# Pairwise channel-layer tails, a residual turned by DMA, and a bias-on-TensorE first batch in an attention and MLP-mixer kernel

## The chip, the core and the metric

The kernel runs on one core of one Trainium2 chip. The metric is device time in microseconds (us) of one execution; ten runs of the kernel before have a median of 291.51 us (290.18 to 292.82). Engines: PE is TensorE (matrix products into PSUM), ACT is ScalarE, DVE is VectorE, POOL is GpSimd, SP is SyncE. Loads that cast f32 to bf16 are issued by POOL, plain and transposing DMAs by SP.

## What is computed

For each of 8 batches: sliding-window attention with a linear distance bias (8 heads of 64, 576 positions, a window of 128), then one mixer block over tokens and one over channels.

```python
scores = scale * q @ k.T                                  # 8 x 576 x 576 a batch
bias = slopes[h] * -abs(i - j); mask = (0 <= i - j < 128)
attn = softmax(where(mask, scores + bias, -1e9))
x = (attn @ v) laid out as [576, 512]
u = x + (relu(x.T @ w_tok1) @ w_tok2).T                   # 576 -> 256 -> 576
out = u + relu(u @ w_ch1) @ w_ch2                         # 512 -> 1536 -> 512
```

## The kernel before, in words

**Tiling.** The 576 positions of a batch are four blocks of 128 and a tail of 64. The softmax needs no maximum: the scores are exponentiated on ACT (`pe`), and DVE multiplies them by `masks`, which holds exp(-slope * distance), zero outside the window (`pb`). A 65th column of ones in the values (`vp`) gives the row sums.

**Work items.** Each item is a small function with a one-letter name, and strings of names (PROLOGUE, FIRST, SECOND, PERIOD, LAST) set by hand the order in which every engine gets its instructions. A prime moves an item to the next batch. Names that are used below:

- `l`, `q`: loads of k and q of batches 0 and 1 (batch 0's heads 0 to 3 by SP as f32, cast by DVE in `cq` and ACT in `ck`; the rest by POOL); `v0` to `v4`: values; `LW`: the token weights W1, W1t, W2; `G0` to `G2`, `H0`, `H1`: the channel weights WC1 and WC2.
- `A0` to `A3`, `AT`: q and k of two heads, or of the tail, transposed on PE into `psM` banks (line 229), and copied out by DVE and ACT (line 234). Later batches are transposed by DMA (`Zq`, `Zk`).
- `S<kb><j>`: scores of key block kb for four heads (lines 308 to 317), their exponential on ACT (line 322, 279 for the half items `s`, `t`) and the mask product on DVE (lines 282, 329, 333, 338). Score matmuls use 64 of the 128 array rows, two heads at a time.
- `P`: attention times values and the normalising; in batch 0 `p0` to `p3`, each for two heads. `k`, `u`, `x` in batch 0 (`K`, `U`, `X` elsewhere): first token layer, second token layer with residual, transpose for the channel layers. `UT`: the tail of the second token layer, into `utt` (channels x 64 positions for each batch of a pair).
- `C0` to `C11`: first channel layer, one 128-wide block of the 1536 each (line 501, four matmuls of 512 columns), ReLU on DVE (line 504) or ACT (line 507). `C` needs every `x` of its batch.
- `T0`, `T1` (lines 510 to 521): the same layer for the 64-position tail, six blocks each, in **every** batch: 24 matmuls with 64 columns into the single bank `psT`, then one ReLU on ACT (line 519).
- `D<c><part>`: second channel layer for 128 positions, in three parts of four matmuls (line 549), a DVE add of the residual (line 554) and the store. `E0` to `E2`: the same for the two tails of a pair of batches together (line 571); at its end four matmuls against the identity (line 575) bring the residual from `utt`, and ACT copies the bank out (line 579).
- `M0` to `M3`: the mask tables (two ACT exponentials each, line 703); `W<n>`: n warm-up matmuls on zeros (line 687); `e1`, `e2`, `ek`, `ex`: constants in buffers, written by ACT.

**Order and rotation.** PSUM holds two double banks `psS` (scores and P), three banks `psM` in rotation (A, C, D, E, K, U, X, some S of batch 0), and `psT`. Each engine takes its instructions in the order of the strings, so an instruction that waits holds back what stands behind it. POOL issues its DMAs in that order too, and each waits until the eighth one before it has landed.

Of the kernel before, what the change touches and what calls it, by code (L numbers as in the profile page):

```python
# [10 lines left out]
ACT = mybir.ActivationFunctionType  # L11
# [8 lines left out]
U_ACT = (0, 1, 3)  # L20
# [3 lines left out]
l0 I W2 q0 q1 J M3 l1 ck0 M0 W3 M1 W3 W3 l23 cq0 O qt m0 A0 q23 W3 v3 v0 ck1 v1 M2 FC W1 cq1 A1  # L24
s0 v2 S20 A2 t0 AT S10 A3 W2 S30 W2 S11 l01' v4 S01 q01' LW ex p0 G0 p1 W1 S21 m1 k0 S31 k1 q23'
l23' A1' e1 qt' W2 v4' ek p2 u0 A0' p3 G1 k2 S00' LC G2 u1 v1'
"""
FIRST = """
H1 v3' k3 u2 v2' x0 u3 A3' v0' W1 H0 A2' Lk'' UT x2 x1 AT' Lq'' S20' x3 Zq'' Zk'' Lk''' T0 S10'
S01' v3'' v0'' Lq''' C9 v0''' S21' C11 v4'' C3 e2 S31' C0 C5 S30' C7 C8 S11' C10 E0 C1 C2 v2''  # L30
C4 P2' v4''' C6 P3' D00 P0' P4' T1 E2 v1'' P1' D01 D02 K0' K1' D10 U1' v2''' D11 D12 U2' UT'
Zq''' X1' U0' U3' D20 D30 S11'' S20'' v1''' D21 D31 E1 Zk''' S00'' D22 S01'' D32
"""
SECOND = """
T1 X2 X0 X3 S30' S31' T0 C8 C9 C7 C11 C2 P0' C5 Lk''' C3 v0''' C4 v1''' C1 S21' S10' C10 Lq'''
v2''' v3'' C0 P4' C6 D00 P3' D01 v3''' P1' P2' D02 K0' S20'' K1' v4''' S01'' D10 D11 D12 U1' U0'
UT' U2' U3' X0' S21'' S11'' D20 D21 X3' S10'' S00'' E0 E1 D22 E2 X2' D30 D31 X1' D32 P0''
"""
PERIOD = """
C3 C7 Zq'' S31' S30' C10 C1 Zk'' C8 P1' C6 T1 P2' C11 P4' C2 C4 P3' C9 Lk''' v4''' C0 C5 K0'  # L40
S00'' K1' S01'' D00 v0''' D01 D02 U2' T0 Lq''' v1''' U1' U0' UT' U3' P0'' D20 X3' v2''' X2'
v3''' X0' D10 X1' D21 D22 S11'' S10'' D11 D30 D31 E0 D12 D32 E1 E2 S21'' S20''
"""
LAST = """
C8 C0 C3 C4 C7 C11 T1 C10 C9 T0 C6 C2 C1 C5 D00 E0 D01 D02 D10 D11 E1 D20 D12 E2 D21 D30 D31 D22
D32
# [3 lines left out]
SPLIT = (1, 2)  # L50
S_M = (0, 2, 4, 5, 6)
S_P = ()
x_DVE = (1, 2, 3)
k_DVE = (2,)
AK_DVE = (2, 3, 7)
AQ_ACT = (1, 3, 4, 5, 7)
DVE_RELU = (2, 3, 4, 5, 7, 8, 10, 11)
# [3 lines left out]
def kernel(  # L61
# [31 lines left out]
    def T(name, shape, dt=bf16):  # L93
        return sb.tile(shape, dt, name=name, tag=name)
# [11 lines left out]
    def S2():  # L106

        t = psS[srot[0] % 2]
        srot[0] += 1
        return t  # L110
# [12 lines left out]
    dist = T("dist", [P, 2, P], f32)  # L123

# [32 lines left out]
    r2t = [T(f"r2t{i}", [P, NHT, 2, ST]) for i in range(2)]  # L157
    ob = [T(f"ob{i}", [P, DM], f32) for i in range(4)]
# [5 lines left out]
    def later(n, fn):  # L164
        pend.append([n, fn])
# [98 lines left out]

    def score_half(kb, a):

        def f():
            if a == 0:
                n = qrot[0]
                qrot[0] += 1  # L270
                half[kb] = (S2(), pe[n % len(pe)], pb[n % len(pb)])
                probs[0, kb, 0] = half[kb][2]
            s, e, p = half[kb]
            cs = slice(a * 256, (a + 1) * 256)
            for h in range(2):
                r = slice(h * D, (h + 1) * D)
                nc.tensor.matmul(s[:, h, cs], lhsT=kT[0][r, kb, a, :],
                                 rhs=qT[0][r, kb:kb + 2, a, :], start=True, stop=True)
            nc.scalar.activation(out=e[:, :, cs], in_=s[:, :, cs], func=ACT.Exp, scale=scale)

            def g():
                nc.vector.tensor_tensor(
                    out=p[:, :].rearrange("p (h x) -> p h x", h=2)[:, :, cs], in0=e[:, :, cs],
                    in1=masks[:, 0, :, a].rearrange("p h g x -> p h (g x)"), op=ALU.mult)
            later(MASK_LATER, g)
        return f
    tok1_banks = {}

    def score(b, kb, j):
# [4 lines left out]

        def f():
            n = qrot[0]
            qrot[0] += 1
            apart = j * 4 + kb in (S_M if b == 0 else S_P if b > 2 else ())
# [20 lines left out]
            split = apart or b == 0 and j * 4 + kb in SPLIT  # L319
# [6 lines left out]
            def g():  # L326
                if kb < NC - 1:
                    for h in (parts if b == 0 else (slice(0, 2),)):
                        nc.vector.tensor_tensor(  # L329
                            out=p[:, :].rearrange("p (h x) -> p h x", h=2)[:, h], in0=e[:, h, :],  # L330
                            in1=masks[:, j, h].rearrange("p h g a x -> p h (g a x)"), op=ALU.mult)
                    return
                nc.vector.tensor_tensor(
                    out=p[:, 0:512].rearrange("p (h g x) -> p h g x", h=2, g=2),
                    in0=e[:, :, 0:256].rearrange("p h (g x) -> p h g x", g=2),
                    in1=masks[:, j, :, :, 0, :], op=ALU.mult)

                nc.vector.tensor_tensor(
                    out=p[:, 512:1024].rearrange("p (u h x) -> p h u x", u=4, h=2),
                    in0=e[:, :, 256:512].rearrange("p h (u x) -> p h u x", u=4),  # L340
                    in1=maskt[:, j].rearrange("p h t g x -> p h (t g) x"), op=ALU.mult)
            later(MASK_LATER, g)
        return f
# [166 lines left out]
    def ch1_tail(b, g, n=6):  # L510
        def f():
            for j in range(n):
                ht = g * n + j
                o = psT[:, j * ST:(j + 1) * ST]
                for cb in range(NCB):
                    nc.tensor.matmul(o, lhsT=WC1[:, cb, ht * P:(ht + 1) * P],  # L516
                                     rhs=utt[(b // 2) % 2][:, cb, b % 2, :],
                                     start=(cb == 0), stop=(cb == NCB - 1))
            nc.scalar.activation(out=r2t[(b // 2) % 2][:, g * n:(g + 1) * n, b % 2, :],  # L519
                                 in_=psT[:, 0:n * ST].rearrange("p (j x) -> p j x", j=n),  # L520
                                 func=ACT.Relu)
        return f
# [36 lines left out]
    def ch2_tail(b, parts=2):  # L559

        st = {}
        pi2 = (b // 2) % 2

        def part(pi):
            def f():
                if pi == 0:
                    st["t"] = M()
                t = st["t"]
                n = NHT // parts
                for ht in range(pi * n, (pi + 1) * n):  # L570
                    nc.tensor.matmul(t[:, :], lhsT=r2t[pi2][:, ht, :, :], rhs=WC2[:, ht, :],  # L571
                                     start=(ht == 0), stop=False)
                if pi == parts - 1:
                    for cb in range(NCB):
                        nc.tensor.matmul(t[:, cb * P:(cb + 1) * P], lhsT=utt[pi2][:, cb, :, :],
                                         rhs=ident[:, :], start=False, stop=(cb == NCB - 1))
                    o = ob[orot[0] % len(ob)]
                    orot[0] += 1
                    nc.scalar.copy(out=o[:, :], in_=t[:, :])
                    for i in range(2):  # L580
                        nc.sync.dma_start(out=out[b - 1 + i, SM:S, :], in_=o[i * ST:(i + 1) * ST, :])
            return f
        return [part(i) for i in range(parts)]
# [107 lines left out]
    def ones_v(i):  # L691
        nc.vector.memset(vp[i][:, :, :, D:D + 1], 1.0)
        nc.vector.memset(vp[i][ST:P, NC, :, 0:D + 1], 0.0)
# [28 lines left out]

    def load_wc1(g):
        nc.gpsimd.dma_start(
            out=WC1[:, :, g * 512:(g + 1) * 512],
            in_=moe_w_ch1[:, g * 512:(g + 1) * 512].rearrange("(j p) h -> p j h", p=P))

    def first_constants():
        nc.vector.memset(kT[0][:, NC, :, ST:P], 0.0)
        nc.vector.memset(hm[:, :], 0.0)  # L730
        nc.vector.memset(hm[0:D, 0:1], 1.0)
        nc.vector.memset(hm[D:P, 1:2], 1.0)
# [5 lines left out]
    def fill_v(i):  # L738

        nc.scalar.activation(out=vp[i][:, :, :, D:D + 1].rearrange("p c h o -> p (c h o)"),  # L740
                             in_=zt[:, 0:(NC + 1) * H], func=ACT.Copy, bias=1.0)
        nc.scalar.copy(out=vp[i][ST:P, NC, :, 0:D + 1],
                       in_=zt[ST:P, None, 0:D + 1].broadcast_to([ST, H, D + 1]))

    def fill_k1():
        nc.scalar.copy(out=kT[1][:, NC, :, ST:P], in_=zt[:, None, 0:ST].broadcast_to([P, NHP, ST]))

    def fill_x1():
        nc.scalar.copy(out=xt[1][:, :].rearrange("p (a x) -> p a x", a=4),
                       in_=zt[:, None, :].broadcast_to([P, 4, P]))  # L750
# [16 lines left out]
    def names(b):  # L767
# [16 lines left out]
        for g in range(2):  # L784
            d[f"T{g}"] = ch1_tail(b, g)
# [22 lines left out]
        if b == 0:  # L808
# [13 lines left out]
            d["e1"], d["e2"] = lambda: fill_v(1), lambda: fill_v(2)  # L822
# [3 lines left out]
            d["LW"] = load_w12  # L826
            d["O"] = lambda: ones_v(0)
# [57 lines left out]
```

The softmax here doesn't subtract the row's maximum and nothing guards it: scores larger than these inputs give would overflow.

## Time and profile before

| | |
|---|---|
| median of ten runs | 291.51 us |
| the profiled execution | 291.71 us, span 290.0 us |
| mean granted PE clock | 0.994 |
| DVE busy | 177.4 us (61%), 348 instructions |
| ACT busy | 115.3 us (40%), 176 instructions |
| line 501 (C), line 549 (D) on PE | 384 and 372 matmuls, 90.2 and 86.5 us |
| line 516 (T) on PE | 384 matmuls of 64 columns, 13.8 us |
| line 687 (warm-up) on PE | 23 matmuls, 8.9 us |
| POOL's DMA queue | 17.41 MB, 78.2% of 16 DMA engines' span |
| first matmul of C | 35.30 us after the span's start |

Busy time counts each instruction from its start to its modelled end; matmuls overlap, so on PE the distance from one start to the next says more than the mean duration. Items have no names in the profile: they are found by line, by tile and by order. The chain that ended last goes back from the last instruction, at each step to what released it.

### The profile page before, as it was taken

The numbers are of one execution on the slowest core, as the hardware profiler recorded it, in microseconds if no ns is written. First come the engines' busy times: TensorE is split into PE (matmuls) and PEld (weight loads), VectorE is DVE, ScalarE is ACT, GpSimd is POOL, SyncE is SP. The second block draws the span as 40 slices with busy tenths as digits, with TensorE's granted clock in tenths as the row PEclk, the third lists the DMA queues.
The fourth block names the chain that finished last, engine by engine and source line by source line (L and its number), as shares of the span: only waits on it lengthen the run. The fifth ranks groups of instructions, "written<-read, shape, count | busy, mean of one in ns | idle before, by whom it ended". The sixth has DMA issues, their size and how long they took to land.

```text
span 290.0 us, 6456 instructions
## 1 busy us (share of the span) xinstructions
PE 281.1 (97%) x2707; PEld 155.5 (54%) x2707; DVE 177.4 (61%) x348; ACT 115.3 (40%) x176; POOL 99.4 (34%) x128
## 2 busy tenths in 40 slices
PE   8769999999999999999999999999999999999995
PEld 3348746546465556644655456644655456645543
DVE  3795687557687578456856467557846476426212
ACT  5878782137224632425341262435241263101300
POOL 8866543089319604920195006910000000000000
PEclk9998999999999999999999999999999999999999
DMA  7999999799999988997599679996703320051004
GB/s 176 165 199 193 198 184 139 152 161 140 149 184 153 171 205 109 138 182 158 125 123 169 125 178 116 139 161 159 128 2 90 98 67 2 36 111 72 2 36 145
DMA packets 148636, 38.00 MB, mean 131 GB/s; under 512 B 135808, under 2 KB 144128, under 8 KB 148608
## 3 DMA queue, kind: packets, MB, share of 16 engines
q0 software_dynamic: 103152, 17.41, 78.2%
q1 hardware_dynamic: 45456, 20.19, 30.4%
q8 instruction: 21, 0.34, 0.5%
q14 instruction: 7, 0.06, 0.1%
HBM read 35.85 MB, written 9.44 MB: 156 GB/s over the span
## 4 chain that ended last, share of the span: by engine, by line
PE 90%; DMA 4%; DVE 3%; issue 1%; POOL 1%; ACT 0%; SPq 0%
PE psM L501 29%; PE psM L549 28%; PE psM L434 4%; PE psM L459 4%; PE psS L308 4%; PE psT L516 4%; PE psM L571 4%; DMA W<-in_moe_w_tok_dram 3%; PE psS L373 2%; PE psS L369 2%; PE psS L401 1%; DMA qf<-in_q_dram 1%; PE psS L312 1%; PE psM L530 1%; PE psM L229 1%
## 5 line engine op out<-in xcount | busy, mean ns | idle before, releaser
L501 PE MATMUL psM<-utb,WC 128*128 128x512 bf16 x384 | 90.2, 379 | 0.0
L549 PE MATMUL psM<-WC,r 128*128 128x512 bf16 x372 | 86.5, 379 | 0.0
L322 ACT ACTIVATE pe<-psS 128x1024 bf16<-128x1024 f32 (+1 forms) x60 | 58.5, 1011 | 50.6 <-PE psS L308 44.3
L549 PEld LDWEIGHTS <-r 128*128 128x128 bf16 x372 | 34.5, 98 | 40.8 <-issue 3.2
L501 PEld LDWEIGHTS <-WC 128*128 128x128 bf16 x384 | 34.5, 97 | 37.7 <-issue 1.9
L504 DVE TENSOR_SCALAR r<-psM 128x512 bf16<-128x512 f32 x64 | 43.4, 687 | 15.0 <-PE psM L501 14.5
L185 POOL DMA_DIRECT2D kn<-in_k_dram x24 | 21.0, 893 | 80.0 <-DMA kT<-kn 75.1
L329 DVE TENSOR_TENSOR pb<-pe,masks 128x1024 bf16<-128x1024 bf16 (+1 forms) x52 | 32.8, 638 | 22.9 <-ACT pe L322 22.0
L554 DVE TENSOR_TENSOR ob<-psM,ub 128x512 f32<-128x512 f32 x31 | 21.4, 691 | 32.1 <-PE psM L549 32.0
L507 ACT ACTIVATE r<-psM 128x512 bf16<-128x512 f32 x32 | 19.1, 598 | 54.4 <-PE psM L501 53.8
L185 POOL DMA_DIRECT2D vp<-in_v_dram x32 | 29.2, 965 | 2.1 <-DMA WC<-in_moe_w_ch_dram 1.5
L185 POOL DMA_DIRECT2D qn<-in_q_dram x24 | 21.4, 947 | 3.4 <-DMA WC<-in_moe_w_ch_dram 2.9
L383 DVE TENSOR_TENSOR xb<-psS,rt 128x512 bf16<-128x512 f32 x28 | 19.4, 692 | 1.0
L461 DVE TENSOR_TENSOR ub<-psM,xb 128x512 bf16<-128x512 f32 x28 | 18.0, 685 | 2.1 <-PE psM L459 1.8
L373 PE MATMUL psS<-vp,pb 128*128 128x65 bf16 x224 | 15.7, 193 | 0.0
L373 PEld LDWEIGHTS <-pb 128*128 128x128 bf16 x224 | 13.6, 97 | 3.3
L459 PE MATMUL psM<-r,W 128*128 128x512 bf16 x56 | 15.4, 379 | 0.0
L516 PEld LDWEIGHTS <-WC 128*128 128x128 bf16 x384 | 13.2, 98 | 3.1
L519 ACT ACTIVATE r2t<-psT 128x384 bf16<-128x384 f32 x16 | 7.9, 491 | 17.4 <-PE psT L516 16.8
L308 PE MATMUL psS<-qT,kT 64*128 64x256 bf16 x172 | 14.5, 272 | 0.0
L516 PE MATMUL psT<-utt,WC 128*128 128x64 bf16 x384 | 13.8, 193 | 0.0
L434 PE MATMUL psM<-xb,W 128*128 128x256 bf16 x112 | 13.4, 273 | 0.0
(125 smaller groups left out, 294.4 us busy)
## 6 DMA issues: line engine op xcount, KB each, us to landing
out_dram<-ob SPq DMA_DIRECT2D x31, 256.0 KB, 2.2
vp<-in_v_dram POOLq DMA_DIRECT2D x32, 128.0 KB, 5.7
kn<-in_k_dram POOLq DMA_DIRECT2D x24, 128.0 KB, 4.3
qn<-in_q_dram POOLq DMA_DIRECT2D x24, 128.0 KB, 4.7
WC<-in_moe_w_ch_dram POOLq DMA_DIRECT2D x3, 512.0 KB, 9.2
WC<-in_moe_w_ch_dram POOLq DMA_DIRECT2D x2, 768.0 KB, 13.2
out_dram<-ob SPq DMA_DIRECT2D x10, 128.0 KB, 2.3
ks<-in_k_dram POOLq DMA_DIRECT2D x3, 256.0 KB, 6.4
```

Source lines behind the costliest of these rows:

```text
L185: nc.gpsimd.dma_start(out=dst, in_=src[b, :, c * P:(c + 1) * P, :].rearrange("h s d -> s h d"))
L308: nc.tensor.matmul(s[h][:, a * 256:(a + 1) * 256], lhsT=kT[i][r, kb, hp, :], rhs=qT[i][r, kb:kb + 2, hp, :], start=True, stop=True)
L322: nc.scalar.activation(out=e[:, h, :], in_=s[n][:, None, :] if split else t2[:, :, :], func=ACT.Exp, scale=scale)
L329: nc.vector.tensor_tensor(out=p[:, :].rearrange("p (h x) -> p h x", h=2)[:, h], in0=e[:, h, :], in1=masks[:, j, h].rearrange("p h g a x -> ...
L373: nc.tensor.matmul(ov, lhsT=prob(b, qb, h, 0), rhs=vt[:, qb, h, 0:D + 1], start=first, stop=(hh == 3))
L434: nc.tensor.matmul(st["t"][h][:, dh * 256:(dh + 1) * 256], lhsT=W1[:, c, dh * P:(dh + 1) * P], rhs=by_half(xb[b % 2][:, c, :])[:, h], star ...
L459: nc.tensor.matmul(t[:, :], lhsT=W2[:, j, c * P:(c + 1) * P], rhs=r1[b % 2][:, j, :], start=(j == 0), stop=(j == 1))
L501: nc.tensor.matmul(t[:, :], lhsT=WC1[:, cb, ht * P:(ht + 1) * P], rhs=utb[b % 2][:, :, cb, :], start=(cb == 0), stop=(cb == NCB - 1))
L504: nc.vector.tensor_scalar(out=r2[b % 2][:, ht, :], in0=t[:, :], scalar1=0.0, scalar2=None, op0=ALU.max)
L516: nc.tensor.matmul(o, lhsT=WC1[:, cb, ht * P:(ht + 1) * P], rhs=utt[(b // 2) % 2][:, cb, b % 2, :], start=(cb == 0), stop=(cb == NCB - 1))
L549: nc.tensor.matmul(t[:, :], lhsT=r2[b % 2][:, ht, c * P:(c + 1) * P], rhs=WC2[:, ht, :], start=(ht == 0), stop=(ht == NHT - 1))
L554: nc.vector.tensor_tensor(out=o[:, :], in0=t[:, :], in1=ub[b % 2][:, c, :], op=ALU.add)
```

## The change

- **Tails.** `T` exists only for odd batches, in three groups of four blocks, and each matmul takes the tails of both batches of the pair as 128 columns; the group fills the whole bank `psT`.
- **Residual.** For the pairs that end in batches 3, 5 and 7 the item `Y` turns `utt` by a DMA transpose on SP into `ut2`, and `E2` ends with a DVE add of `ut2`; the four identity matmuls and ACT's copy stay only in batch 1.
- **Batch 0.** DVE casts the distance table to bf16 (`distb`) and scales the identity by each head's slope (`sid`, eight instructions), in item `B`. Each score bank first gets `sid @ distb` (bias and mask) on PE, then the scores are accumulated on it, and ACT's exponential writes `pb` directly: batch 0 has no mask product on DVE. `M` is therefore needed only for batch 1 on, and `m`, `M` move back. More of the batch's exponentials are split by head, and S30 goes in four pieces.
- **Engines.** `e1`, `e2`, `ek`, `ex` and first constants go from ACT and DVE to POOL; in `C` the ReLUs on DVE go from eight to five blocks of twelve (the rest on ACT); copies after `A` and `x`, and the token ReLU of `k`, are dealt out anew; `u2` also adds its residual on PE.
- **Orders.** All five strings are new. In the prologue, `LW` stands before the loads of batch 1's q and k (it stood behind the first of them), the second f32 load is of k, the item S00 is whole and kb 1 is in halves (`s1`, `t1`), 20 warm-up matmuls instead of 23, and `C` begins with C5 rather than C9. `T0` of the first pair comes at the end of FIRST.

```diff
-U_ACT = (0, 1, 3)
+U_ACT = (0, 1, 2, 3)
-SPLIT = (1, 2)
-S_M = (0, 2, 4, 5, 6)
+SPLIT = (0, 1, 3, 5, 6)
+S_M = (2, 4, 5, 6)
+Y_DMA = (3, 5, 7)
-DVE_RELU = (2, 3, 4, 5, 7, 8, 10, 11)
+DVE_RELU = (4, 5, 7, 8, 10)
...
+    def bias(out, h, d, first=True):
+        nc.tensor.matmul(out, lhsT=sid[:, h, :], rhs=d, start=first, stop=False)
...
+            for n, (a, cs, d, _, _) in enumerate(todo):
+                for h in range(2):
+                    bias(s[h][:, cs], 2 * (2 * j + a) + h, d, n == 0)
+            for n, (a, cs, _, kk, qs_) in enumerate(todo):
+                for h, r in enumerate(halves):
+                    nc.tensor.matmul(s[h][:, cs], lhsT=kT[0][r, kk, 2 * j + a, :], rhs=qs_[r],
+                                     start=False, stop=(n == len(todo) - 1))
...
-    def ch1_tail(b, g, n=6):
+    def ch1_tail(b, g, n=4):
...
-                    nc.tensor.matmul(o, lhsT=WC1[:, cb, ht * P:(ht + 1) * P],
-                                     rhs=utt[(b // 2) % 2][:, cb, b % 2, :],
-                                     start=(cb == 0), stop=(cb == NCB - 1))
+                    nc.tensor.matmul(psT[:, j * P:(j + 1) * P], lhsT=WC1[:, cb, ht * P:(ht + 1) * P],
+                                     rhs=utt[pi2][:, cb, :, :],
+                                     start=(j == 0 and cb == 0), stop=(j == n - 1 and cb == NCB - 1))
...
+            nc.sync.dma_start_transpose(
+                out=ut2[pi2][:, :, :], in_=utt[pi2][:, :, :, :].rearrange("p c i x -> p (c i x)"))
...
+                    if b in Y_DMA:
+                        nc.vector.tensor_tensor(out=o[:, :], in0=t[:, :],
+                                                in1=ut2[pi2][:, :, :].rearrange("p c x -> p (c x)"),
+                                                op=ALU.add)
...
+    def make_bias():
+        nc.vector.tensor_copy(out=distb[:, :, :], in_=dist[:, :, :])
+        for h in range(H):
+            nc.vector.tensor_scalar(out=sid[:, h, :], in0=ident[:, :], scalar1=-float(slopes[h]) / scale,
+                                    scalar2=None, op0=ALU.mult)
...
-        for g in range(2):
-            d[f"T{g}"] = ch1_tail(b, g)
+        if b % 2:
+            for g in range(3):
+                d[f"T{g}"] = ch1_tail(b, g)
+            if b in Y_DMA:
+                d["Y"] = utail_trans(b)
```

The prologue's string before and after:

```
l0 I W2 q0 q1 J M3 l1 ck0 M0 W3 M1 W3 W3 l23 cq0 O qt m0 A0 q23 W3 v3 v0 ck1 v1 M2 FC W1 cq1 A1
s0 v2 S20 A2 t0 AT S10 A3 W2 S30 W2 S11 l01' v4 S01 q01' LW ex p0 G0 p1 W1 S21 m1 k0 S31 k1 q23'
l23' A1' e1 qt' W2 v4' ek p2 u0 A0' p3 G1 k2 S00' LC G2 u1 v1'

W4 O J I W3 l0 B W3 ck0 q0 l1 q1 l23 FC cq0 W1 q23 v4 A0 qt v2 v0 W3 ck1 cq1 s1 A1 v1 S00 t1 S20
W2 A3 v3 LW A2 AT S11 l01' S30 q01' ek ex S21 M3 p0 l23' LC q23' G0 p1 M1 S01 k0 S31 u0 p2 M2 k1
p3 qt' G1 M0 A1' A0' m0 W2 A2' u1 v2' e1 A3' e2 v4' S00'
```

## The prediction

> **What bounds the kernel now.** I read the busy times first, then the same engines by stretches of the span, then the start in stretches of one clock window, then the chain that ended last. Columns of the stretches: length, busy us and instructions of PE, PEld, DVE, ACT, POOL, granted clock, DMA share, GB/s.
>
> ```profile
> PE 281.1 (97%) x2707; PEld 155.5 (54%) x2707; DVE 177.4 (61%) x348; ACT 115.3 (40%) x176; POOL 99.4 (34%) x128
> ```
>
> ```profile
> 8.00:35.30 27.30, 22.74 (x392) 16.51 (x393) 19.82 (x53) 21.90 (x44) 19.50 (x26) 0.94 1.58 191
> 35.30:286.70 251.40, 251.40 (x2286) 136.39 (x2284) 154.01 (x283) 88.77 (x124) 72.75 (x87) 1.00 1.06 123
> ```
>
> From the first C (35.30 us) to the last matmul PE never stops: there only PE work counts, and ACT is busy 88.77 of 251.40 us. Before 35.30 PE is idle at times and ACT is busy 21.90 of 27.30 us: there the time is set by waits. So the change is two sums: PE work after the first C, and the moment at which C starts.
>
> ```profile
> 17.28:20.69 3.41, 1.67 (x25) 0.88 (x23) 3.21 (x13) 1.66 (x4) 2.05 (x4) 1.00 1.29 202
> 20.69:24.10 3.41, 3.41 (x40) 2.42 (x41) 1.44 (x5) 2.92 (x6) 2.11 (x3) 0.50 1.36 199
> ```
>
> A stretch with PE busy 1.67 of 3.41 us, most of it a wait for W1, is followed by 3.41 us at half clock. The chain names that load, and gives the pace of matmuls (start, us, what):
>
> ```profile
> 11.96 7.69 DMA W<-in_moe_w_tok_dram
> ...
> 53.16 1.75 PE psM L434 x16
> ...
> 59.52 0.86 PE psM L459 x4
> ...
> 62.11 0.54 PE psS L308 x8
> ...
> 67.08 0.70 PE psT L516 x24
> 67.78 0.67 PE psM L491 x12
> ```
>
> So a matmul with 512 columns costs 216 ns, 256: 109, 128: 56, 64: 29. Score matmuls (64 rows, two heads at once) cost half, 55 ns for 256 columns, and 95 ns more on entering and on leaving a group of them: 8 x 55 + 95 = 0.54.
>
> **After the first C (PE's sum).**
>
> *Tails.* Before, 384 matmuls of 29 ns, 11.2 us; after, 192 of 56, 10.75. Halving the count gains little, since the columns stay the same. Before's C start has T0 of batch 0 behind it (24 x 29 = 0.70) and the new one has none, so behind C it is 360 x 29.2 = 10.51 against 10.75: **+0.24**, with the 0.70 credited to the start below. The Trainium skill, "TensorE: Matmul & The Clock Gate", section "Back-to-back issue gap", gives about 81 ns a matmul for streams of weight load and matmul at 128 columns; if the weight load also held a 64-column matmul at 81 ns, merging would save 192 x 81 ns, 15.6 us by estimate. The chain's 29 and 56 ns contradict that here, and I go by them.
>
> *Residual.* Three of four pairs lose four 128-column matmuls: 12 x 56 = **-0.67**. E2's DVE add (0.69, line 554) replaces ACT's copy (0.585, line 579); both engines have room behind C. The transpose is not in the trace; the rows nearest in size land in 2.5 us (kT<-knt, half as large) and 4.4 us (utb<-ub, twice as large). Y stands on SP behind Zk, with the next stores queued behind it; E2 comes at the period's end, some 25 us later, and in LAST 12 matmul groups of 0.86 (10 us) later. That hides it; if not, DVE waits with stores and PSUM releases behind it, and each us late is a us lost.
>
> *Score groups.* Behind C the orders have 62 changes between 64- and 128-row matmuls before and 58 after: 4 x 95 ns = **-0.38**. One score item of kb 3 (0.25) has moved ahead of C and one of 0.44 behind it, with small change left: **-0.03**.
>
> *PSUM waits.* T now drains 512 columns (0.59, against 0.49 on line 519) between T0 and T1; P2 and P4 between them give 16 x 29 + 8 x 58 ns = 0.93, and matmul to ACT takes 0.26, so 0.90 is needed: just hidden, up to 0.3 in all if ACT is late. ReLUs on ACT rise by 3 x 8 x 0.6 = 14 us on top of 88.77 in 251: hidden. Right after C5 the scores S30 and S01 need psS banks whose exponentials (0.92 apart) end about 36.4, while PE is there at 35.6: **+0.65**, against 0.15 of such gaps in the trace before: **+0.50** net.
>
> Sum behind C: 0.24 - 0.67 - 0.38 - 0.03 + 0.50 = **-0.34**.
>
> **Up to the first C.** PE gets 16 + 8 bias matmuls of 256 columns, 8 of 128 and 16 of 64: 24 x 109 + 8 x 56 + 16 x 29 = 3.5 us, and 0.22 for u2. DVE loses 16 mask products of about 0.42. ACT loses fills of 0.62 + 0.41 + 0.63 + 0.40 = 2.1 us (to POOL), gains three copies or ReLUs and two pieces (about 1.9), and its eight mask exponentials (0.33 each) leave the idle time before 9 us for the middle of the chain. ACT now paces the start:
>
> ```profile
> 8.35 0.72 ACT L703 ACTIVATE masks<-dist 128x256 bf16<-128x256 f32 x2
> ...
> 10.30 1.11 ACT L322 ACTIVATE pe<-psM 128x512 bf16<-128x512 f32 x2
> ...
> 14.38 1.02 ACT L322 ACTIVATE pe<-psS 128x1024 bf16<-128x1024 f32 x1
> ```
>
> Two 512-column pieces take 1.11, so 0.49 each back to back; 1024 columns about 0.92, copies of 512 about 0.49, mask rows 0.33. With 0.3 us from a matmul to ACT or DVE, and 0.05 back, I walk the new order:
>
> - The 11 warm matmuls still hold A0 to 5.86. DVE's new distb and sid (0.35, then 8 x about 0.15, bounds 0.1 and 0.4 by the DVE rows of 64 and 256 columns) end near 5.0, before the cast that A0 needs must run; at the high end A0 slips 0.8, but A1 waits for the fourth f32 load anyway.
> - A1 ends 9.2 as before, its copies 10.05. Exponentials of S00, t1, S20 from 10.55 to 13.1; copies of A3, A2, AT to 15.0; S11 from 15.75, S30 in four pieces to 18.05. p0 can end only then, at 18.2 (before: 16.96).
> - p0's DVE work is 1.35, so k0 runs 19.6 to 20.2, as before (19.70), though W1 is no longer what it waits for: two loads of 256 KB, 1.3 us each, now stand behind it, and POOL's new fills (0.2 for the 128-column row, so perhaps 0.8 for the large one) cost it under 1 us.
> - Four mask rows hold ACT for 1.3, so u0 waits for its ReLU until 21.75; p2, k1, p3 follow to 24.0; A1' and A0' wait for ACT behind the last masks until 25.6; then PE is nearly full: A2', u1, A3', S00' to 28.3, k3, x0, k2, S20' to 30.3, AT', u3, u2, UT, x2 to 33.7, S10', S31' to 34.25. ACT's copy of x2 ends 34.55.
>
> So C5 starts at **34.6**, against 35.30 with T0's 0.70 in it: the bias work is covered by waits that were there, but nothing else is won: **-0.70**. The later loads are not bare: WC1's last third, which C11 needs at 36.2, landed at 33.08 before and now has one more load of 128 KB (0.85) ahead; batch 1's q and k are needed at 24.0, some 1 us after they should land. If that 1 us is gone, PE waits the difference.
>
> **Sum.** 291.71 - 0.70 - 0.34 = 290.67 for the profiled execution; it stood 0.20 above the median, so **290.4** beside the median of 291.51. A measurement here tells 0.3%, 0.9 us, from no change; the forecast lies just beyond it.
>
> **The clock.** The walk has no PE gap over 0.85 us and therefore takes full clock. By the rows above a window with 1.67 us of PE work is followed by a slow one. The Trainium skill, "TensorE: Matmul & The Clock Gate", section "HAM oscillation — how this bites in real kernels", asks for gaps of over 3.4 us; by it the old kernel, whose longest gap was 1.65, would have had no slow window. The row decides: one such window in the new start would cost PE up to 1.7 us.
>
> **Rivals.**
> - *The start closes up (289.0).* ACT's queue from 8 to 34.6 holds 22.4 us of work by the paces above, so 4.2 us of its gaps are in my walk. If a third to a half of them close (p0's last scores, the copies of A), C5 comes at 33.2: 1.4 us more. For it: PE no longer runs at half clock there. Against: each bank of psM waits for ACT in turn.
> - *Nothing is left (291.5).* A slow clock window or a late load costs about 1.1 in the start and the sum is gone. For it: DMA queue 0 at 78%; against: the margins above.
> - *Slower (292.9).* ACT, place: S00 to S30 and the masks. If its instructions follow at their durations (0.6) rather than at 0.49, 33 of them by 34.6 us come 3.6 us later, some 2.5 of it on the path: C5 at 37.1. It decides from C5 at 35.6 (no gain) and 36.5 (slower beyond the 0.3%). Against: the 1.11 for two.
>
> **Chances.** Forecast 0.45 (own range 289.8 to 291.1, 0.33 of it under 290.64), start closes up 0.25, nothing left 0.15, slower 0.15. So faster 0.33 + 0.25 = 0.58, same 0.12 + 0.15 = 0.27, slower 0.15. The range takes the rivals in, less the far ends: 288.5 to 292.6.
>
> **What would show it.** Line 565 with 192 starts 56 ns apart; line 640 with 4 matmuls; first C at 34.6, its wait ended by ACT; k0 at 19.6 released by DVE, not by W1; half-clock window gone; PE full from 36.7 on. Wrong if C5 starts outside 33 to 36.5, if PE waits for WC1, or if DVE waits for Y.

## The result and the profile after

The changed kernel takes **293.01 us** in the median of 15 runs (292.03 to 297.22); the kernel before, run beside it, 290.91 us (52 runs). The ratio is **1.0076** (95% interval 1.0057 to 1.0095): slower by some 0.8%, where 290.4 us beside 291.51 had been forecast, faster by 0.4%. Medians here and below are of all runs; the ratios leave out runs in a slower state of the chip, so the two can differ a little. The profiled execution took 293.41 us, span 291.4; that of before 291.71 and 290.0. (Of the experiments below, the profiled executions of `tail2_in_even`, `v_after_x` and `tails_each_mended` lie 1.9, 1.1 and 4.4 us above the medians of their kernels and that of `v_after_x_mended` 1.1 below, so that only medians are compared there.)

The same views as before: the busy times, then the two stretches, cut at the new first C (32.87) and the new last matmul.

```profile
PE 281.0 (96%) x2552; PEld 156.0 (54%) x2552; DVE 157.3 (54%) x310; ACT 124.9 (43%) x195; POOL 103.4 (35%) x140
```

```profile
8.00:32.87 24.87, 22.75 (x407) 16.77 (x404) 12.27 (x34) 21.76 (x50) 20.89 (x31) 1.00 1.60 179
32.87:287.60 254.73, 250.98 (x2101) 136.03 (x2096) 141.07 (x261) 99.39 (x140) 75.55 (x91) 1.00 1.08 126
```

The first row is the good half: the first C comes 2.43 us earlier, at full clock throughout. The second is where the time went. Before, PE was busy 251.40 of 251.40 us behind the first C; now 250.98 of 254.73. The view of PE's waits names what came in (us in total, times, longest):

```profile
PE psM L548 <- DMA utb<-ub: 2.3, 2, 1.2
PE psT L750 <- DVE zt L745: 1.1, 1, 1.1
PE psM L234 <- DMA qs<-in_q_dram: 1.0, 2, 0.5
PE psS L356 <- ACT pe L370: 0.5, 1, 0.5
...
PE psM L548 <- DMA WC<-in_moe_w_ch_dram: 0.4, 1, 0.4
PE psM L538 <- DVE ob L612: 0.4, 1, 0.4
PE psM L548 <- ACT utb L541: 0.2, 1, 0.2
```

The rows of `zt` and `qs` belong to the start. The others lie behind the first C, and the first is the largest: C (line 548) waits twice for the transposing DMA that item X issues. The chain that ended last shows one of them (start, us, what); no `utb` DMA is in the chain of the kernel before.

```profile
123.41 1.57 PE psM L607 x8
124.97 8.50 DMA utb<-ub
133.48 0.14 issue
133.61 1.89 PE psM L548 x8
```

8.50 us for a DMA that the prediction took at 4.4. The view of the tile `utb` on SP sums up all ten (issue to landing), first in the kernel before, then in the changed one:

```profile
DMA to landing us min/median/max: 3.1/4.4/5.8
```

```profile
DMA to landing us min/median/max: 3.1/4.6/8.5
```

The median is the same; two pairs of them became slow. These lie at the end of the periods of batches 2 and 4. Here are the last 12 us of the first of these periods, before and after (columns as above; the last two are the DMA share and GB/s):

```profile
122.00:126.00 4.00, 4.00 (x58) 2.52 (x57) 3.69 (x8) 0.86 (x2) 3.03 (x4) 1.00 2.09 178
126.00:130.00 4.00, 4.00 (x25) 1.76 (x24) 1.37 (x2) 0.77 (x1) 0.00 (x0) 1.00 1.70 168
130.00:134.00 4.00, 4.00 (x24) 1.79 (x24) 2.27 (x4) 1.17 (x2) 0.00 (x0) 1.00 0.40 110
```

```profile
122.00:126.00 4.00, 4.00 (x36) 2.04 (x33) 3.01 (x6) 0.37 (x1) 3.60 (x5) 1.00 2.02 184
126.00:130.00 4.00, 4.00 (x25) 1.76 (x24) 2.08 (x3) 1.94 (x2) 0.00 (x0) 1.00 2.13 137
130.00:134.00 4.00, 2.86 (x19) 1.07 (x18) 2.25 (x4) 1.94 (x2) 0.00 (x0) 1.00 1.46 218
```

The DMA engines are loaded from 126 to 130 in both, but in the changed kernel they move fewer bytes (137 against 168 GB/s), are still at work after 130, and PE is busy only 2.86 of the last 4 us. The single DMAs tell why. Before, the last value load (`vp`) was issued at 124.03 and the two transposes at 125.86 and 127.16, landing 4.7 and 4.2 us later. After, the transposes go out at 123.64 and 124.97, between value loads of 122.86, 123.73 and 124.60; the transposes take 8.0 and 8.5 us and the loads 7.1 to 8.4 (4.8 to 5.5 before; those of batch 7, 6.0 to 6.5).

The **account**, profile against profile; a gap is the time between two matmuls' starts beyond what the first costs at the prediction's paces:

| | forecast | measured |
|---|---|---|
| start of the first C | -0.70 | 32.87 - 35.30 = -2.43 |
| PE's work behind it | -0.84 | -0.97 |
| PE's gaps behind it | +0.50 | 4.85 - 0.36 = +4.50 |
| last matmul to end of span | 0 | +0.29 |
| span | -1.04 | +1.39 |

The new gaps are 2.62 (the transposes), 1.32 in three places behind C5 (0.15, 0.69, 0.48), 0.51 (an X item behind a bank that DVE drains, line 612), 0.23 (C behind ACT's copy of an x), and 0.17 in small ones.

### The profile page after: what moved, and what is told of

Same layout as the page of the kernel before. It is cut to its first block, busy times and chain, and to the rows that moved or that the text cites. A ratio compares the mean times of both kernels' runs of the same rounds, so it can differ in the third digit from the quotient of the medians.

```text
span 291.4 us, 6153 instructions
## 1 busy us (share of the span) xinstructions
PE 281.0 (96%) x2552; PEld 156.0 (54%) x2552; DVE 157.3 (54%) x310; ACT 124.9 (43%) x195; POOL 103.4 (35%) x140
## 4 chain that ended last, share of the span: by engine, by line
PE 80%; DMA 10%; POOL 8%; issue 1%; DVE 0%; ACT 0%; POOLq 0%
PE psM L548 29%; PE psM L607 24%; DMA utb<-ub 6%; PE psM L481 4%; PE psM L506 4%; DMA WC<-in_moe_w_ch_dram 4%; PE psT L565 4%; PE psM L629 4%; PE psS L356 3%; PE psS L420 2%; PE psS L416 2%; POOL vp L190 2%; PE psS L448 1%; POOL qkt L193 1%; PE psM L588 1%
## 5 line engine op out<-in xcount | busy, mean ns | idle before, releaser
L370 ACT ACTIVATE pe<-psS 128x1024 bf16<-128x1024 f32 x56 | 54.5, 1026 | 42.1 <-PE psS L356 41.8
L548 PEld LDWEIGHTS <-WC 128*128 128x128 bf16 x384 | 35.3, 98 | 41.9 <-issue 3.9
L554 ACT ACTIVATE r<-psM 128x512 bf16<-128x512 f32 x56 | 33.3, 598 | 55.3 <-PE psM L548 55.3
L376 DVE TENSOR_TENSOR pb<-pe,masks 128x1024 bf16<-128x1024 bf16 x42 | 28.9, 689 | 27.5 <-ACT pe L370 27.5
L551 DVE TENSOR_SCALAR r<-psM 128x512 bf16<-128x512 f32 x40 | 27.4, 688 | 16.6 <-PE psM L548 16.2
L420 PE MATMUL psS<-vp,pb 128*128 128x65 bf16 x224 | 15.7, 193 | 0.0
L429 DVE RECIPROCAL rt<-psS 128x8 f32<-128x8 f32 x28 | 5.7, 204 | 17.0 <-PE psS L420 17.0
L506 PE MATMUL psM<-r,W 128*128 128x512 bf16 x56 | 14.5, 379 | 0.0
L356 PE MATMUL psS<-qT,kT 64*128 64x256 bf16 x168 | 13.3, 272 | 0.5 <-ACT pe L370 0.5
L416 PE MATMUL psS<-vp,pb 128*128 128x65 bf16 x168 | 12.9, 193 | 0.0
L565 PEld LDWEIGHTS <-WC 128*128 128x128 bf16 x192 | 11.6, 98 | 2.3 <-issue 0.2
```

The source lines that it names most:

```text
L356: nc.tensor.matmul(s[h][:, a * 256:(a + 1) * 256], lhsT=kT[i][r, kb, hp, :], rhs=qT[i][r, kb:kb + 2, hp, :], start=True, stop=True)
L370: nc.scalar.activation(out=e[:, h, :], in_=s[n][:, None, :] if split else t2[:, :, :], func=ACT.Exp, scale=scale)
L376: nc.vector.tensor_tensor(out=p[:, :].rearrange("p (h x) -> p h x", h=2), in0=e[:, :, :], in1=masks[:, j].rearrange("p h g a x -> p h (g a ...
L420: nc.tensor.matmul(ov, lhsT=prob(b, qb, h, 0), rhs=vt[:, qb, h, 0:D + 1], start=first, stop=(hh == 3))
L506: nc.tensor.matmul(t[:, :], lhsT=W2[:, j, c * P:(c + 1) * P], rhs=r1[b % 2][:, j, :], start=(j == 0), stop=(j == 1))
L548: nc.tensor.matmul(t[:, :], lhsT=WC1[:, cb, ht * P:(ht + 1) * P], rhs=utb[b % 2][:, :, cb, :], start=(cb == 0), stop=(cb == NCB - 1))
```

## The experiments

**The theory.** T has left the periods of batches 2 and 4 (before: 48 matmuls of 29 ns there, 1.4 us). X therefore goes out earlier after the period's first C (20.87 us instead of 22.55), while the loads of the batch after next, which wait for the transposes of k, go out later (10.27 instead of 9.14; this second part varies by the execution: with T in every batch they went out between 8.66 and 12.34 us after the first C of the periods of batches 2 and 4). The transposes meet the value loads, both share the DMA engines, and C waits. **Rivals:** Y, the new DMA on SP, delays the queue; E, which stands in the tail's period, is what matters; or the loss is in the start and around C5, not there at all.

**`tails_each`**: T for each batch again, everything else as changed.

```diff
-    def ch1_tail(b, g, n=4):
+    def ch1_tail(b, g, n=6):
...
-        if b % 2:
-            for g in range(3):
-                d[f"T{g}"] = ch1_tail(b, g)
+        for g in range(2):
+            d[f"T{g}"] = ch1_tail(b, g)
```

> The changed kernel with the first channel layer's tails done again in every batch (two groups of 24 matmuls of 64 columns), everything else as changed. Theory (period balance): sharing the tails takes 1.4 us of TensorE work out of the periods of batches 2 and 4, so their transposes of u by DMA start while the next batch's loads still run, land late, and C waits 1.30 and 1.32 us. Then here both waits of line 548 for utb fall under 0.4 us, the tail matmuls cost 0.5 us more, and the time falls by about 2.1 us, to 290.9. Rival (the start and the bias work cost the time): no change of more than 0.7 us, 293 to 293.7, waits gone or not.

292.23 us, ratio 1.0037 (1.0013 to 1.0062): 0.8 us less than the changed kernel, but not the 290.9 that was expected. No wait for `utb` is left in its profile, and the gaps fall from 4.85 to 2.74, although a new one has come in (0.72, an X item behind a bank); the first C came 0.59 later. PE's work behind the first C is 0.49 us more; 384 x 29.2 ns against 192 x 56 ns makes 0.46. So, between these two profiles, merging the tails saves half a microsecond of PE and brings 2.6 of waits; the rest of the loss is elsewhere. The transposes are not fast here either:

```profile
DMA to landing us min/median/max: 3.1/5.5/8.0
```

Those of batch 4 took 7.6 and 6.8 us and landed 0.4 us before C needed them. What this kernel has is enough time, and not by much.

**`pair_tails_only`**: the kernel before with the merged tails alone (T2 behind C5, C9 and C2 in the last three strings).

```diff
-        for g in range(2):
-            d[f"T{g}"] = ch1_tail(b, g)
+        if b % 2:
+            for g in range(3):
+                d[f"T{g}"] = ch1_tail(b, g)
```

> The kernel before with one part of the change alone: the first channel layer's tails by pair (three groups of 128-column matmuls in odd batches). Theory (period balance): TensorE work falls by 0.5 us in all, but 1.4 us leave the periods of batches 2 and 4, where the transposes landed only some 0.7 to 1.3 us ahead of C; C waits about 0.5 to 1.3 us in each, and the time is 291 to 292.3, not faster than the 290.9 of before. Rival (the tails are a plain gain and the loss lies elsewhere): 290.4 or less, with no wait for utb.

293.0 us, 1.0062 (1.0029 to 1.0095): this part alone makes the old kernel slower, and lands above the 291 to 292.3 expected. A wait for `utb` (0.7) has come in, with transposes of 7.2 and 7.4 us, and one of 0.65 in the period of batch 0, which lost its T as well: there P waits for a score bank that DVE drains. PE's work behind the first C rises by 0.10, against +0.24 forecast.

**`no_late_v`**: the changed kernel without six value loads, those of batches 5 and 7 that meet the transposes. It leaves these loads out; the products use old values.

```diff
-            d[f"v{c}"] = lambda c=c: load_v(b, c)
+            if not (b in (5, 7) and c in (0, 1, 2)):
+                d[f"v{c}"] = lambda c=c: load_v(b, c)
```

> The changed kernel without three of the five value loads of batches 5 and 7 (its output for these batches is made from old values): these are the loads that run beside the transposes of u in the periods of batches 2 and 4. If it is the sharing of DMA engines that makes those transposes land 8.0 and 8.5 us after issue instead of about 4.5, they land in 5 us or less here and the two waits of 1.3 us go: 290.4. If their lateness has another cause (order on SP, the tail's transpose), the waits stay and the time is 293.

290.12 us, 0.9981 (0.9955 to 1.0008). The same two views in this run:

```profile
DMA to landing us min/median/max: 3.1/4.5/5.9
```

```profile
122.00:126.00 4.00, 4.00 (x27) 1.96 (x26) 2.61 (x6) 0.30 (x1) 0.16 (x1) 1.00 1.90 188
126.00:130.00 4.00, 4.00 (x26) 1.74 (x24) 2.08 (x3) 1.94 (x2) 0.00 (x0) 1.00 0.97 168
130.00:134.00 4.00, 4.00 (x37) 1.74 (x37) 2.65 (x5) 2.10 (x3) 0.00 (x0) 1.00 0.17 66
```

The transposes land in 5.1 and 4.5 us, PE is full, the periods of batches 2 and 4 take 29.54 us instead of 30.84 and 30.86, and the other gaps stay. The value loads are what slows the transposes, and this costs 2.6 to 2.9 us: more than the whole loss. Without these six loads, which the kernel before does have, the changed kernel comes to parity.

**`residual_on_pe`**: the identity matmuls again for all pairs, no Y.

```diff
-Y_DMA = (3, 5, 7)
+Y_DMA = ()
```

> The changed kernel with the tails' residual brought in by the four identity matmuls and ACT's copy for all pairs (no transpose of the tail by DMA). Theory (period balance): the tail's transpose lies in the odd periods, where nothing waits for it; taking it away leaves both waits of 1.3 us for utb and adds 12 matmuls of 56 ns, 0.7 us: 293.5. Rival (the extra transposes on SP slow the queue): the waits for utb shrink and the time falls below 292.5.

292.26 us, 1.0061 (1.0033 to 1.0089). The first wait stays (1.21), so Y isn't its cause. PE's work rises by 0.73, near the forecast's 0.67. The second wait is gone here, with transposes of 6.9 and 6.4 us. Y is no likely cause of that one either: in the changed kernel's trace it goes out at 140.47 and 207.76 us and lands within 3 us, while the waits end at 133.61 and 199.28, so it is in flight in neither.

**`tail2_in_even`**: E0 to E2 of a pair in the following period, ahead of C5 and K0.

```diff
-        if b % 2:
-            for i, f in enumerate(ch2_tail(b, CH2_PARTS)):
+        if b == B - 1 or b % 2 == 0 and b:
+            for i, f in enumerate(ch2_tail(b if b % 2 else b - 1, CH2_PARTS)):
```

> The changed kernel with the second channel layer of a pair's tails (three groups, 2.6 us of TensorE) moved from the odd period into the even one that follows, ahead of the token layers. Theory (period balance): no work is added or removed, the even periods get 2.6 us more before u is made, the loads are over when the transposes start, and both waits for utb go: 293.0 - 2.6 = 290.4. Rival (the waits come from the transposes themselves or from the stores, or the loss lies in the start): 293.0.

294.79 us, 1.0141 (1.0099 to 1.0183): slower. The waits for `utb` are gone as meant, but where E ended, a K item now waits for E2's bank (0.73, 0.84, 0.84), and where E left, a D part waits for the bank of the one before (1.36):

```profile
PE psM L481 <- DVE ob L635: 1.3, 2, 0.7
PE psM L607 <- DVE ob L612: 1.2, 1, 1.2
```

Cover is not the only thing that an item gives to its neighbours; its place in the rotation of three banks is another.

**`balanced`**: the same move, but E ahead of C0, with C4 and C7 between the scores behind C5, UT of the next batch ahead of X1, D22 ahead of S10.

```diff
-S31' v0''' C5 v4'' S30' S01' v3'' v0'' C11 C8 C9 S21' S11' E2 C3 C10 C4 Lq''' v1'' v2'' P4' C1
+S31' v0''' C5 v4'' C4 S30' C7 S01' v3'' v0'' C11 C8 C9 S21' S11' C3 C10 Lq''' v1'' v2'' P4' C1
...
-C7 Zq'' C3 S30' S31' C8 Zk'' C11 C6 Y C1 T0 P2' P4' T1 C4 C2 Lk''' P1' C10 C9 T2 P3' C0 C5 K0'
+C7 Zq'' C3 S30' S31' C8 Zk'' C11 C6 Y C1 T0 P2' P4' T1 C4 C2 Lk''' P1' C10 C9 T2 P3' E0 E1 E2 C0 C5 K0'
```

> The changed kernel with orders mended where its trace shows waits, all work kept: the second channel layer's tails of pairs 1 and 3 and 5 move into the following even period, ahead of two C groups; behind C5 two more groups of C come before the scores that wait for PSUM; the second token tail goes between U and X of batch 1; T0 of the first pair behind the last transposes. Theory: waits of line 548 for utb (2.6 us), of the scores and WC1 near 34 us (1.3), of X at 56 us (0.4) and of C at 66 us (0.2) go: 293.0 - 4.5 = 288.5, faster than both kernels. Rival (the waits only move, to PSUM banks or later loads): 291 or more, with new waits of TensorE.

290.57 us, 0.9991 (0.9971 to 1.001): 2.4 us less than the changed kernel. The three gaps around C5 are gone from its profile. It stays at parity and does not reach the 288.5 expected: one wait for `utb` (0.7, transposes of 7.6 and 8.0 us) and one for a bank (0.6) are left.

**`fills_after_loads`**: POOL's constants (O) behind its first loads. This asks whether they hold back the f32 load that the first scores need.

```diff
-W4 O J I W3 l0 B W3 ck0 q0 l1 q1 l23 FC cq0 W1 q23 v4 A0 qt v2 v0 W3 ck1 cq1 s1 A1 v1 S00 t1 S20
+W4 J I W3 l0 B W3 ck0 q0 l1 q1 l23 FC cq0 W1 q23 O v4 A0 qt v2 v0 W3 ck1 cq1 s1 A1 v1 S00 t1 S20
```

> The changed kernel with POOL's two fills of the first value buffer moved behind its first two casting loads, so that the first of these is issued near 2.6 us (as before the change) rather than 3.53. Theory for the start (it is paced by the fourth f32 load, which landed at 6.64 after and at 7.80 before, because the casting load started 0.95 us later): the fourth f32 load lands near 7.8, the second pair of transposes starts near 8.5 instead of 7.17, and C starts about 1 us later, 33.9; time +0.5 to +1. Rival (the start is paced later, by the q and k loads of heads 4 to 7 at 11.1, or by ACT): C starts at 32.9 or earlier, time unchanged.

293.37 us, 1.0087 (1.0059 to 1.0115). A miss: the fourth f32 load landed at 6.94, not at the 7.8 that both the prediction and this theory held for. A1 came 0.44 later, yet k0 began at 18.13 as in the changed kernel, so A1 doesn't pace that stretch. The first C did come at 33.80, next to the 33.9 expected, but that is luck: PE waited 1.4 us for q of batch 1 instead.

**`w1_late`**: the token weights (LW) behind the loads of batch 1's first q and k, nearly as before.

```diff
-W2 A3 v3 LW A2 AT S11 l01' S30 q01' ek ex S21 M3 p0 l23' LC q23' G0 p1 M1 S01 k0 S31 u0 p2 M2 k1
+W2 A3 v3 A2 AT S11 l01' S30 q01' LW ek ex S21 M3 p0 l23' LC q23' G0 p1 M1 S01 k0 S31 u0 p2 M2 k1
```

> The changed kernel with the token weights loaded behind batch 1's first q and k loads again. Theory: W1 lands near 20.3 instead of 17.6, the first token layer (18.13 after) waits some 2 us for it, and C starts 1.5 to 2 us later than 32.9: time +1.5 to +2, and a half-clock window may come back. Rival (the early load of W1 buys nothing, since ACT paces the start): C moves by less than 0.5 us.

294.11 us, 1.0107 (1.0067 to 1.0148). W1 landed at 20.15 instead of 17.61, k0 waited 2.2 us, and the first C came at 34.42, 1.55 later. The order of these loads is worth that in the new start. No half-clock window followed this wait. It lies across two of the 3.41 us windows of the clock's record in this trace (the last section comes back to them):

```profile
15.59:19.00 3.41, 2.46 (x45) 1.67 (x44) 2.07 (x8) 3.41 (x11) 3.14 (x6) 1.00 1.44 194
19.00:22.42 3.42, 2.08 (x41) 1.77 (x42) 0.75 (x3) 1.37 (x4) 2.69 (x4) 1.00 1.35 199
22.42:25.83 3.41, 3.14 (x83) 2.91 (x79) 2.24 (x8) 3.41 (x10) 3.24 (x7) 1.00 1.36 202
```

**`v_after_x`**: all loads kept, but the three value loads held on POOL until the transposes have landed.

```diff
-S01'' S00'' K1' D00 v3''' v4''' D01 Lq''' D02 U2' U0' UT' U3' v1''' U1' P0'' D20 v2''' D21 D10
-v0''' X2' X3' X1' X0' D22 S10'' S11'' D30 D11 D31 D12 E0 S20'' S21'' D32 E1 E2
+S01'' S00'' K1' D00 v3''' v4''' D01 Lq''' D02 U2' U0' UT' U3' U1' P0'' D20 D21 D10
+X2' X3' X1' X0' Q' v1''' v2''' v0''' D22 S10'' S11'' D30 D11 D31 D12 E0 S20'' S21'' D32 E1 E2
...
+        d["Q"] = lambda: nc.gpsimd.tensor_copy(
+            out=held[:, 0:2].rearrange("p (c x) -> p c x", c=2), in_=utb[b % 2][:, 0:4:2, 0, 0:1])
```

> The changed kernel, with the last three value loads of every period held back on POOL until the transposes of the token result that C waits for have landed (a copy of two of their columns into a small tile makes POOL wait); all work is kept. If those transposes are late because they share the DMA engines with these loads, the two waits of 1.3 us and the longer even periods go as in the run that left the loads out: they land in about 4.5 us instead of 8, periods 4 and 6 fall from 34.81 towards 33.5, 293.0 - 2.6 = 290.4. Rival: the queue has no room for it, the loads then land late and the transposes of q and k behind them, or P, wait: the wait moves and the time stays near 293.

291.12 us, 1.0012 (0.9993 to 1.0031): 1.9 of the 2.6 us come back, with all the work done. (The expectation names the wrong periods: 34.81 is the length of those of batches 3 and 5; those with the wait should fall from 30.8 to 29.5. That of batch 4 did, to 29.55.) In the profiled execution the first wait stayed, at 1.7: there the second period's loads were late already, and the transposes met q's loads instead (9.5 and 8.5 us). By the median the queue has room for the move; in this execution it had not.

**`v_after_x_mended`**: the same, with FIRST's order of `balanced`.

> The same, and in the string of the first period C4 and C7 between the score items that waited for a bank behind C5, and UT before X1. In the run that had this string, with other edits beside it, the gaps of 0.69, 0.48, 0.51 and 0.23 us near C5 and X were gone. If they are lost on PE's own time they come off in full: another 1.5 to 1.9 us less, about 288.7, which would be under the kernel before by 0.7%. Rival: only the place of the waits changes, the time is that of the run without the reorder.

292.09 us, 1.0025 (0.9997 to 1.0054). A miss. In its profile the gaps around C5 are gone, but a wait for `utb` is left (0.9, transposes of 8.8 and 8.2 us, again among q's loads), and 0.5 us of a wait for a value load has come into the second period. That execution took 291.0; what makes the median no better than without the reorder isn't settled.

**`tails_each_mended`**: `tails_each` with the same two moves in FIRST, and T0 of batch 1 between D32 and the X items that waited for a bank.

```diff
-U0' Zk''' D20 D30 D21 E1 D31 X2' UT' D22 S00'' D32 X0'
+U0' Zk''' D20 D30 D21 D31 X2' D22 S00'' D32 T0' X0'
```

> The changed kernel with tails for each batch (no collision of transposes and loads), and the string of the first period mended: C4 and C7 between the score items behind C5, UT of the next batch before X1, and T0 of batch 1 between D32 and the last X items, where X3 waited 0.72 us for a bank. The run with tails for each batch had 2.74 us of PE gaps behind the first C, 2.4 of them at these places. If PE's own work sets the rest, they come off in full: 292.2 - 2.2 = 290.0, at or just under the kernel before (290.9). Rival: as in the run with held loads and the same reorder, items that come earlier wait for what they need, a value load or a bank, and the gaps move: 291.5 to 292.

290.41 us, 0.9981 (0.996 to 1.0002): 1.8 less than `tails_each`. Of the kernels that do all the work it comes nearest to beating the kernel before; its interval still reaches 1. In the profiled execution the gaps behind C5 and at X are gone (0.17 is left of the latter). It is the longest of the 13 runs, with a mean clock of 0.992, and it has two waits for `utb`, 2.7 and 0.5 us, the first with a half-clock window behind it. T stands in every batch here; but the loads went out late against PE (12.34 and 11.30 us after the first C of the two periods), and X ahead of the last value load. So the collision can come back without merged tails; this one execution doesn't tell how often.

**`before_again`**: the kernel before, profiled a second time.

> The kernel before once more, unchanged: does the start repeat from execution to execution? If the half-clock window and the landing of W1 at 19.65 us belong to the kernel, the first C starts at 35.3 again, within 0.2 us. Rival: they belong to the one execution, and C starts between 34.5 and 35.5 with or without the window.

The first C came at 35.72, 0.4 later, and the fourth f32 load landed at 7.21 instead of 7.80. This time PE did not wait for W1 but 1.8 us for a converted q (`qs`), whose f32 load was late, and the half-clock stretch lay earlier (from 10.8 to 17.6, instead of 20.69 to 24.10):

```profile
6.00:13.00 7.00, 3.88 (x48) 2.15 (x46) 4.62 (x15) 4.18 (x11) 6.39 (x9) 0.84 1.90 167
13.00:20.00 7.00, 6.42 (x79) 3.19 (x77) 4.95 (x14) 5.41 (x11) 4.46 (x7) 0.67 1.53 193
```

Which load is late differs between two executions of one kernel, and so does the place of the window; the first C came within 0.4 us all the same.

## Why the prediction was wrong

**The step that failed** is its first: "From the first C (35.30 us) to the last matmul PE never stops: there only PE work counts", used for the changed kernel as for the old one. A stretch without gaps says that each wait there has some margin, not how much. The prediction gave the tails as a sum of PE work, +0.24, and allowed for waits at PSUM banks (+0.50), but asked of no transfer in the periods of batches 2 and 4 what a shorter period does to it. It looked at POOL's queue only for the start, and at `utb<-ub` only for a price of Y, with the 4.4 us of its row. The margin was there to read: in the trace before, the second transpose landed at 131.35 and C started at 134.25, 2.9 us; the last value load was issued 1.8 us before the first transpose.

T stood ahead of X. Taking its 1.4 us out moves X and the C that needs it up together, and the margin stays (2.8 us in `no_late_v`). What moves is X against the loads, which POOL issues in its own time: the transposes now go out among them and take twice as long, 4 us more against a margin of 2.8. Nine profiles have all loads and either kernel's own order in the periods of batches 2 and 4, which makes 18 such periods. With T in every batch X went out 0.8 us behind the last value load on average (8 periods), with merged tails 0.6 us ahead of it (10). In the ten periods where X was over 0.1 us ahead, eight of them with merged tails, the transposes took 7.0 to 9.9 us and C waited each time; in the other eight they took 4.2 to 7.6, and it never did. `no_late_v` shows the price (2.9 us at the medians), and `tails_each` and `pair_tails_only` show that the tails are the part of the change that brings it.

Two of the prediction's own signs of being wrong came true in the changed kernel, but not at the place of this loss: C5 started outside 33 to 36.5, and PE waited for WC1.

**The other terms.**

- *Tails' pace: right.* Line 565 has its 192 matmuls; they start 56 ns apart, so 16 take 0.90 us, and `tails_each` confirms the difference in the sum (0.49). At the 81 ns of the Trainium skill, "TensorE: Matmul & The Clock Gate", section "Back-to-back issue gap", 16 would take 1.30 by estimate; the measurement decides against it for streams of this form.
- *Residual: right.* Line 640 has 4 matmuls; the transposes of Y land in 2.5 to 3.0 us; no wait of DVE for them is in the trace; `residual_on_pe` measures 0.73 for the forecast 0.67.
- *PE's work in all: right*, -0.97 against -0.84.
- *Waits around C5: right place, half the size.* 0.65 forecast for the scores behind C5; 0.69 measured on the bank (line 356 behind ACT's exponential), but 0.48 more before the next C, part of it for the third piece of WC1, which landed at 35.61. The prediction had that piece needed at 36.2 and asked whether PE would wait for it; with C5 1.7 us earlier than forecast, it did.
- *X behind a bank (0.51), C behind ACT's copy (0.23): not foreseen.* In `balanced` and `tails_each_mended` UT stands ahead of X1, and the first falls to 0.16 and 0.17.
- *The start: mis-sized, in the good direction.* C5 at 32.87, not 34.6: the rival "the start closes up" came close there (33.2), by another way than it gave, ACT's gaps. The walk took A1's end at 9.2 "as before", but that end belonged to an f32 load that landed at 7.80 in that one execution; in the eleven profiles with the new prologue or a variant of it it landed between 6.23 and 7.11, and in two others of the old one at 7.21 and 6.53. A1 ended 1.4 earlier, k0 began at 18.13 instead of 19.6, and from there DMA paced it: q of batch 1 landed at 24.86, the 1 us margin "gone" as the prediction feared, with 1.0 us of waits (`qs`).
- *The clock: right.* No window at half clock in the profiled execution: the emptiest of its 3.41 us windows before the last matmul has PE busy 2.26 us.

So the start and PE's work gained 3.4 us by the profiles, over twice what had been forecast (the profile of before had a half-clock window in its start, that of after none), and the change still lost: 2.6 us at the transposes, 1.9 net in the other gaps and 0.3 at the end took it all and more. (The prediction's last subtraction, 290.67 - 0.20, makes 290.47 and not 290.4; nothing hangs on it.)

## What to carry to other kernels

An engine that is busy for all of a stretch hides how close its suppliers are. Before work is taken out of such a stretch, read for each transfer in it how long before its use it landed, and which other transfers its new place will meet: what the work gave to its neighbours was time. The margin of one profile isn't enough for that: in `before_again` the same kernel's second transpose of batch 4 landed only 0.6 us before its use. And a start that is measured in one execution carries that execution's late load with it: look at a second before building on its times.

## What the runs showed of the hardware

- A transposing DMA and casting loads in flight together slow each other. `utb<-ub` takes 3.1 to 5.1 us in the periods of batches 5 and 6 (over all profiles), where no load goes out near it, and 7.0 to 9.9 us where it is issued over 0.1 us ahead of a period's last value load; the 128 KB value loads that it meets in the changed kernel take 7.1 to 8.9 us, the same loads before 4.8 to 6.5. In `v_after_x` q's loads did the same to it (8.5 and 9.5 us).
- A half-clock window is a matter of the execution. Of 98 executions of the kernel before that were timed beside the experiments, 37 had a mean clock of 0.998 or more and a median of 290.13 us; the other 61 had 0.988 to 0.994, as the profiled one had, and a median of 291.10. The changed kernel had full clock in 12 of 16, with a median of 292.66. Like with like, at full clock, the change costs 2.5 us, more than the 2.1 of all runs: part of the start's gain was only the window that the profiled execution happened to have.
- By these traces, what decides it is how much of one fixed window PE is busy. In all 14 traces the granted clock changes only at whole multiples of 3.41 us from its first record, and these windows lie differently in each execution (the record begins at 4.90 us in the changed kernel's trace and at 5.35 in that of `w1_late`). With the span cut at these places, five windows before the last matmul have PE busy 1.36 to 1.70 us, in five executions, and each is followed by one at half clock. All others have 1.78 us or more, and full clock follows, but for one in `before_again` that was at half clock itself. The two rows nearest to the limit, in `tail2_in_even` and `fills_after_loads`, each with the window that follows:

```profile
22.84:26.25 3.41, 1.70 (x38) 1.00 (x34) 2.09 (x7) 1.65 (x4) 2.32 (x6) 1.00 1.33 200
26.25:29.66 3.41, 3.41 (x46) 2.51 (x40) 1.07 (x2) 1.75 (x3) 1.72 (x2) 0.50 1.53 192
```

```profile
196.93:200.34 3.41, 1.78 (x10) 0.68 (x9) 2.19 (x4) 1.93 (x2) 0.00 (x0) 1.00 1.92 226
200.34:203.76 3.42, 3.42 (x39) 1.65 (x37) 1.34 (x3) 2.20 (x3) 0.00 (x0) 1.00 1.14 149
```

So the prediction's row (1.67 of 3.41 us, then half clock) is one of five that agree, and the limit here is about half of the window. Whether a wait brings the slow clock depends on where the windows cut it: the 2.2 us of `w1_late` fall into two windows (2.46 and 2.08 us busy) and brought none, the 1.8 us of `before_again` left one with 1.36, the 2.7 us of `tails_each_mended` one with 1.39. The Trainium skill, "TensorE: Matmul & The Clock Gate", section "HAM oscillation — how this bites in real kernels", has gaps over 3.4 us bring the slow clock; no wait here was that long, and windows came all the same.
